# Batch 0's second half of q and k loaded ahead of w_in, transposed before slot 0, and slots 0 to 2 activated on VectorE alone

## The chip, the core and the metric

The kernel runs on one core of one Trainium2 chip. A core has five engines that work side by side and meet at semaphores: TensorE (PE in the profile, with its weight loads as PEld) multiplies matrices into PSUM, VectorE (DVE) and ScalarE (ACT) do elementwise work, GpSimd (POOL) here issues most loads and makes masks, SyncE (SP) issues stores. Loads run on 16 DMA engines that all queues share. The metric is the time of one execution on the device in microseconds (us); before the change its median is 310.11 us over four runs (309.18 to 310.49).

## What is computed

Attention within a band of 32 positions to each side, for 8 batches of 8 heads, 576 positions and head size 64, then a two-layer network with the SMELU activation on the 4608 tokens:

```python
scores = np.matmul(q, k.transpose(0, 1, 3, 2)) / np.sqrt(D)
mask = np.abs(pos[:, None] - pos[None, :]) <= 32
attn = np.exp(np.where(mask, scores, -1e9) - max)      # rows divided by their sums
x = np.matmul(attn, v).transpose(0, 2, 1, 3).reshape(4608, 512)
h = x @ w_in                                           # 512 x 2048
g = np.where(h >= 1, h, np.where(h <= -1, 0.0, (h + 1) ** 2 / 4))
out = g @ w_out                                        # 2048 x 512
```

Inputs and output are float32; the kernel casts q, k, v and the weights to bfloat16 as they are loaded.

## The kernel before

**Slots.** The program is an order written out by hand. After a warm-up comes a loop of slots `a` (L469). A slot takes one block of 256 tokens (`t = a // 8`) and one eighth of the 2048 hidden columns (`f = a % 8`). It multiplies w_in with xT into a PSUM tile `hp` (L491, eight matmuls, called the slot's product here), applies SMELU to hp and writes `gT` (L494 to L503), then does the attention steps listed for this slot (`run(a)`, from the table `ev` that `at` fills, L394 to L413), then one or two pieces of the second layer: a `pair` (L447) or a `quarter` (L431) of eight or four matmuls with w_out. The list `pairs` (L378) gives the slots of the first ten of them.

**SMELU.** With rr = relu(0.5 h + 0.5), slots outside `two_on_act` run rr on ScalarE (L495) and two operations on VectorE, mx = max(h, rr) (L502) and g = min(rr, 1) * mx (L503). Slots in `two_on_act` square rr on ScalarE (L499) and run one operation on VectorE, g = min(max(h, 1), rr^2) (L500). In the first form hp is last read by L502, in the second by L500.

**PSUM.** hp has two buffers in the pool ps_h; slot 6 takes one of ps_o instead (L485). So a slot's product waits until the hp of two slots earlier has been read. ps_s and ps_n have one two-bank buffer each, for scores, sums and transposes. ps_o has two, for the second layer and the last scores of batch 0.

**Attention of a batch.** q and k are loaded by rows and transposed on TensorE for batches 0 and 1 (`tpose`: L187 or L189, and a copy out of PSUM, L190). `scores` multiplies kT with qT (L227; for the first slots a mask is added by L206), and ScalarE takes the exponential (L235, `pt`). `sums` multiplies pt with v and with ones (L293); its `end` takes 1/sum on ScalarE as exp(-ln) (L299 lr, L300 rc), and VectorE's product with it writes xT (L305, L308). These products are put into the list `muls` and are issued at the next `flush()`.

**Warm-up.** q of the first 288 positions comes through SyncE's and ScalarE's queues as float32; everything else comes through GpSimd's queue in the order in which it is issued (L122 to L157). Eight loads may be under way in that queue: each waits for the one eight places before it. The order before is k's first half, v, then line L149: w_in for slots 0 and 1 (`w[:4]`), the second half of q and k (`load_half(1, ...)`), w_in for slots 2 to 6 (columns 1024 to 1536 in two loads of 256 KB, the others in loads of 128 KB); L150: a part of w_out and w_in for slot 7; then three copies on GpSimd that make the masks, used from slot 14 on; more of w_out, and q, k and v of batch 1. The warm-up computes batch 0's scores and sums for the first 256 tokens; `keep_warm` fills in matmuls of zeros. The second half's transposes stand in slot 1 (L394), its scores in slots 2 and 3, its sums in slots 3, 4 and 5.

Of the kernel before, what the change touches and what calls it, by code (L numbers as in the profile page):

```python
# [8 lines left out]
BF = mybir.dt.bfloat16  # L9
AF = mybir.ActivationFunctionType  # L10
ALU = mybir.AluOpType
# [3 lines left out]
def kernel(  # L15
# [20 lines left out]
    B, H, S, D = q.shape  # L36
# [4 lines left out]
    MAIN = 480  # L41
# [13 lines left out]
    ps_h = ctx.enter_context(tc.tile_pool(name="ps_h", bufs=2, space=bass.MemoryType.PSUM))  # L55
    ps_s = ctx.enter_context(tc.tile_pool(name="ps_s", bufs=1, space=bass.MemoryType.PSUM))
    ps_n = ctx.enter_context(tc.tile_pool(name="ps_n", bufs=1, space=bass.MemoryType.PSUM))
# [7 lines left out]
    bias = const.tile([128, 192], BF, name="bias")  # L65
# [8 lines left out]
    V, P, A = nc.vector, nc.gpsimd, nc.scalar  # L74
# [67 lines left out]
    def put(todo):  # L142
        for fn, *x in todo:
            fn(*x)

    w = [(load_w_in, c, c + 256, h) for c in range(0, 1024, 256) for h in range(2)]
    w += [(load_w_in, 1024, 1536, h) for h in range(2)]
    w += [(load_w_in, c, c + 256, h) for c in range(1536, DFF, 256) for h in range(2)]
    put(w[:4] + [(load_half, 1, t, h) for t in range(2) for h in range(2)] + w[4:12])  # L149
    put([(load_w_out, 0, 0, 4)] + w[12:])  # L150
    P.tensor_copy(band[HD[1], 0:128], band[HD[1], 64:192])
    for m, n, x in ((mask4, 8, 128), (mask8, 4, TAIL)):
        P.tensor_copy(m.rearrange("p (n j) -> p n j", n=n),
                      band[:, :x].rearrange("p (n j) -> p n j", n=1).to_broadcast([128, n, x]))
    put([(load_w_out, 0, 4, 8), (load_w_out, 0, 8, 16)] + [(load_rows, 1, t) for t in range(2)])
    put([(load_v, 1, n) for n in range(4)] + [(load_w_out, 1, 8 * n, 8 * n + 8) for n in range(2)])
    put([(load_nat, 2, t) for t in range(2)] + [(load_v, 2, n) for n in range(4)])  # L157

# [3 lines left out]
    def qkT(b, t):  # L162
        if t == 0:
            return qTs[b % 3][:, PAD:]
        if b not in kT:
            kT[b] = ktp.tile([128, NY * S], BF, name="kT")
        return kT[b]

    def tpose(b, n, t, copy, ps):


        half, part = divmod(n, 2)
        j0, j1 = ((0, 5), (5, 9))[part]
        if b:
            src = qn[b] if t == 0 else kn[b]
            src = [src[:, half + 2 * h] for h in range(2)]
            dst = qkT(b, t).rearrange("d (y e p j) -> d y e p j", y=2, e=2, j=9)[:, half, :, :, j0:j1]
            like = "d j (e p) -> d e p j"
        else:
            src = (qn, kn)[t][b, half]  # L180
            src = src if src.shape[1] == 9 else [src[:, h] for h in range(2)]
            dst = qkT(b, t).rearrange("d (y l p j) -> d l y p j", l=2, p=32, j=9)[:, half, :, :, j0:j1]
            like = "d j (p y) -> d y p j"
        for j in range(j0, j1):
            if isinstance(src, list):
                for h in range(2):
                    nc.tensor.transpose(ps[HD[h], j - j0], src[h][:, D * j:D * j + D], ident)  # L187
            else:
                nc.tensor.transpose(ps[:, j - j0], src[:, j], ident)  # L189
        return lambda: copy(dst, ps[:, :j1 - j0].rearrange(like, p=64 if b else 32))  # L190

    def xpose(b, t):

        nc.sync.dma_start_transpose(out=qkT(b, t).rearrange("d (u p) -> d u p", p=128),
                                    in_=(qn, kn)[t][b].rearrange("p u h d -> p (u h d)"))
# [115 lines left out]
    def flush():  # L311
        while muls:
            muls.pop(0)()


    TB = 256

    def tp1(pool):
        if pool is ps_h:
            return pool.tile([128, 8, 128], BF, name="tp", tag="hp")  # L320
        return pool.tile([128, 2, 8, 128], BF, name="tp", tag="bb")[:, 0]
# [10 lines left out]
    def keep_warm(n, pool, tag):  # L332

        z = pool.tile([128, 512], FP, name="z", tag=tag)
        for _ in range(n):
            nc.tensor.matmul(z, warm[:, :128], warm, start=True, stop=True)

    def cast(x, nm, cut):

        y = early.tile([128, 9, 2, D], BF, name=nm)  # L340
        o, i = y.rearrange("p j h d -> p h j d"), x.rearrange("p h (j d) -> p h j d", d=D)
        V.tensor_copy(o[:, :, :cut], i[:, :, :cut])
        A.copy(o[:, :, cut:], i[:, :, cut:])
        return y.rearrange("p j h d -> p j (h d)")

    with tc.tile_pool(name="ps_p", bufs=1, space=bass.MemoryType.PSUM) as ps_p:
        keep_warm(11, ps_h, "hp")

        V.memset(qkT(0, 0).rearrange("d (y s) -> d y s", y=NY)[:, :, S // 2:352], 0.0)
        for b in range(LONG):  # L350
            V.memset(qkT(b, 0).rearrange("d (y s) -> d y s", y=NY)[:, :, S - PAD:], 0.0)
        V.memset(qkT(0, 1).rearrange("d (y s) -> d y s", y=NY)[:, :, S // 2:320], 0.0)
        qn[0, 0] = cast(q32, "qb", 5)
        qq = [tpose(0, n, 0, (A.copy, V.tensor_copy)[n], tp1(ps_h)) for n in range(2)]
        for x in qq:
            x()
        kk = [tpose(0, n, 1, (A.copy, V.tensor_copy)[n], tp1((ps_n, ps_p)[n])) for n in range(2)]
        keep_warm(3, ps_h, "hp")
        for x in kk:
            x()  # L360
        scores(0, (0, 1), (0, 2), (0, 2), None)
        scores(0, (0, 2), (0, 1), (2, 3), None, ps_n, 32)
        scores(0, (1, 2), (0, 2), (0, 2), None, ps_p)
        keep_warm(4, ps_h, "hp")
        e0 = sums(0, 0, 0, TB)
        keep_warm(2, ps_h, "hp")
        e1 = sums(0, 1, 0, TB, ps_p)
        keep_warm(7, ps_h, "hp")
        e0()
        e1()  # L370
    ps_o = ctx.enter_context(tc.tile_pool(name="ps_o", bufs=2, space=bass.MemoryType.PSUM))


# [1 line left out]

    NB = NT // TB
    NF = DFF // 256
    pairs = [(6, 0), (8, 1), (9, 2), (10, 3), (11, 4), (12, 5), (15, 6), (15, 8), (16, 7), (17, 9)]  # L378
    two_on_act = (1, 7, 8, 9, 10, 11, 12)
    ev = {}  # L380

    def at(a, *todo):


        ev.setdefault(a, []).extend(x for x in todo if x)
# [5 lines left out]
                yield (sums, b, y1, lo, hi), (scores, b, (y1, y1 + 1), (0, 2), (2 * k, 2 * k + 2))  # L391
        yield (sums, b, 0, MAIN, S), (scores8, b)

    at(1, (tposes, 0, (0, 1), (1, 1)))  # L394
    at(2, (scores, 0, (0, 1), (0, 2), (2, 4)), (scores8, 0, ps_o))
    at(3, (scores, 0, (1, 2), (0, 2), (2, 4), ps_n), (sums, 0, 0, TB, MAIN, ps_s))
    at(4, (sums, 0, 1, TB, MAIN))
    at(5, (sums, 0, 0, MAIN, S, ps_s))
    seq = [x for b in range(1, B) for x in steps(b, 224)]
    at(13, seq[0][1])  # L400
    at(13.5, (*seq[1][1], ps_n))
    at(14, (*seq[0][0], ps_s), seq[1][0])
    at(16, seq[2][1])
    for n, a in enumerate((18, 20, 22, 28)):
# [10 lines left out]
    for b in range(LONG + 1, B):  # L415
        a = sl[5 * (b - 1) - 7] - 17
# [52 lines left out]
    for a in range(NF * NB + NF):  # L469
        t, f = divmod(a, NF)  # L470
        eng = None if a < 14 else V
        post = [x for n, x in pairs if n == a] + [a - NF] * (a >= 2 * NF + 2)
        for b, x in loads.get(a, []):
            if x < 2:
                load_nat(b, x)
            else:
                for n in range(4):
                    load_v(b, n)
        if a == 0 or a > 3:
            flush()  # L480
        if t < NB:
            if t not in gT:
                gT[t] = gtp.tile([128, 2 * NF, TB], BF, name="gT", tag="gT")
            r0 = TB * t % RING
            if a == 6:  # L485
                hp = ps_o.tile([128, 2, TB], FP, name="hp", tag="op")
            else:
                hp = ps_h.tile([128, 2, TB], FP, name="hp", tag="hp")
            for j in range(2):
                for n, kk in enumerate((0, 2, 1, 3)):  # L490
                    nc.tensor.matmul(hp[:, j], w_in[:, kk, 256 * f + 128 * j:256 * f + 128 * j + 128],  # L491
                                     xT[:, kk, r0:r0 + TB], start=n == 0, stop=n == 3)

            rr = ewp.tile([128, 2, TB], FP, name="rr")  # L494
            A.activation(rr, hp, AF.Relu, scale=0.5, bias=0.5)  # L495
            g = gT[t][:, 2 * f:2 * f + 2]
            mx = ewp.tile([128, 2, TB], FP, name="mx")
            if a in two_on_act:
                A.activation(mx, rr, AF.Square)  # L499
                V.scalar_tensor_tensor(g, hp, 1.0, mx, op0=ALU.max, op1=ALU.min)  # L500
            else:
                V.tensor_max(mx, hp, rr)  # L502
                V.scalar_tensor_tensor(g, rr, 1.0, mx, op0=ALU.min, op1=ALU.mult)  # L503
        flush()
        run(a)
        for x in post:
            (pair if x < 4 * 4 else quarter)(x)
        run(a + 0.5)
        for x in xps.get(a, []):
            xpose(*x)  # L510
# [30 lines left out]
```

The softmax here doesn't subtract the row's maximum and nothing guards it: scores larger than these inputs give would overflow.

## Time and profile before

| What | Value |
|---|---|
| Median of four runs | 310.11 us (309.18 to 310.49) |
| The profiled execution | 310.04 us, of which the span is 308.2 us |
| TensorE busy | 300.3 us (97% of the span) |
| VectorE, ScalarE, GpSimd busy | 242.2, 192.7, 76.8 us |
| Slot 0's product starts | 13.77 us |
| Slot 4's product starts | 23.18 us |
| Granted TensorE clock, mean | 0.997 |

The span runs from the first to the last instruction; the execution has 1.84 us around it. Times below are us from the span's start. In the views a line such as `L491` is a line of the kernel before, `out<-in` are tiles, and a number in brackets is idle time of the engine before the instruction, with what ended it. The rows of digits cut the span into 40 slices of 7.7 us; a digit is the busy share in tenths.

### The profile page before, as it was taken

The numbers are of one execution on the slowest core, as the hardware profiler recorded it, in microseconds if no ns is written. First come the engines' busy times: TensorE is split into PE (matmuls) and PEld (weight loads), VectorE is DVE, ScalarE is ACT, GpSimd is POOL, SyncE is SP. The second block draws the span as 40 slices with busy tenths as digits, with TensorE's granted clock in tenths as the row PEclk, the third lists the DMA queues.
The fourth block names the chain that finished last, engine by engine and source line by source line (L and its number), as shares of the span: only waits on it lengthen the run. The fifth ranks groups of instructions, "written<-read, shape, count | busy, mean of one in ns | idle before, by whom it ended". The sixth has DMA issues, their size and how long they took to land.

```text
span 308.2 us, 8460 instructions
## 1 busy us (share of the span) xinstructions
PE 300.3 (97%) x3634; PEld 205.0 (67%) x3634; DVE 242.2 (79%) x376; ACT 192.7 (63%) x319; POOL 76.8 (25%) x91
## 2 busy tenths in 40 slices
PE   8979999999999999999999999999999999999994
PEld 3558878876666666666666666666666666666651
DVE  4278568978888888889888888889888888887860
ACT  3688786757856667566656666566666666554331
POOL 8798461037009005400460002700000000000000
PEclk9999999999999999999999999999999999999998
DMA  9999999999999989996799055990810001011101
GB/s 153 185 189 193 183 202 154 168 160 158 142 184 111 190 135 98 170 89 145 103 169 142 31 108 89 164 156 17 177 48 36 34 36 36 35 36 40 64 34 68
DMA packets 137013, 35.70 MB, mean 116 GB/s; under 512 B 122128, under 2 KB 132624, under 8 KB 136976
## 3 DMA queue, kind: packets, MB, share of 16 engines
q0 software_dynamic: 102960, 18.06, 82.0%
q1 hardware_dynamic: 33872, 16.81, 24.5%
q8 instruction: 28, 0.46, 0.6%
q10 hardware_dynamic: 144, 0.29, 0.4%
q14 instruction: 9, 0.07, 0.1%
HBM read 36.70 MB, written 9.44 MB: 150 GB/s over the span
## 4 chain that ended last, share of the span: by engine, by line
PE 90%; DMA 4%; POOL 3%; ACT 1%; issue 1%; DVE 0%; POOLq 0%
PE hp L491 39%; PE op L431 37%; PE bb L293 6%; PE op L447 4%; DMA w_in<-in_moe_w_in_dram 4%; PE bb L227 2%; POOL vn L106 1%; POOL w_in L110 1%; PE tp L187 1%; ACT pt L235 1%; POOL kh L85 0%; DVE gT L500 0%; ACT mx L499 0%; PE bb L252 0%; ACT rr L495 0%
## 5 line engine op out<-in xcount | busy, mean ns | idle before, releaser
L491 PE MATMUL hp<-xT,w_in 128*128 128x256 bf16 x1152 | 149.4, 273 | 2.5 <-DVE gT L500 1.1
L495 ACT ACTIVATE rr<-hp 128x512 f32<-128x512 f32 x144 | 85.7, 595 | 88.6 <-PE hp L491 88.6
L491 PEld LDWEIGHTS <-w_in 128*128 128x128 bf16 x1152 | 112.0, 98 | 42.0 <-issue 2.4
L431 PE MATMUL op<-w_out,gT 128*128 128x512 bf16 x512 | 130.4, 380 | 0.0
L502 DVE TENSOR_TENSOR mx<-hp,rr 128x512 f32<-128x512 f32 x137 | 94.5, 690 | 31.6 <-ACT rr L495 29.4
L503 DVE SCALAR_TENSOR_TENSOR gT<-rr,mx 128x512 bf16<-128x512 f32 x137 | 95.2, 695 | 4.7
L431 PEld LDWEIGHTS <-gT 128*128 128x128 bf16 x512 | 47.6, 98 | 36.7
L98 POOL DMA_DIRECT2D qn<-in_q_dram x12 | 14.6, 1224 | 113.1 <-DMA kT<-kn 109.4
L235 ACT ACTIVATE pt<-bb 128x1024 bf16<-128x1024 f32 (+1 forms) x33 | 32.7, 1002 | 4.4 <-PE bb L227 3.0
L305 DVE TENSOR_TENSOR xT<-bb,rc 128x512 bf16<-128x512 f32 (+1 forms) x32 | 21.1, 658 | 10.3 <-ACT rc L300 9.6
L106 POOL DMA_DIRECT2D vn<-in_v_dram x32 | 27.5, 896 | 3.6 <-DMA w_out<-in_moe_w_out_dram 3.3
L436 ACT COPY osb<-op 128x512 f32<-128x512 f32 x32 | 18.7, 583 | 11.8 <-PE op L431 11.3
L300 ACT ACTIVATE rc<-lr 128x512 f32<-128x512 f32 (+2 forms) x40 | 23.5, 587 | 1.3
L299 ACT ACTIVATE lr<-bb 128x512 f32<-128x512 f32 (+2 forms) x40 | 22.1, 551 | 0.4 <-PE bb L293 0.4
L201 DVE TENSOR_TENSOR pt<-pt,mask 128x1024 bf16<-128x1024 bf16 (+1 forms) x33 | 20.3, 614 | 0.2 <-ACT pt L235 0.2
L293 PE MATMUL bb<-pt,ones 64*64 64x256 bf16 (+3 forms) x352 | 19.6, 256 | 0.1
L293 PE MATMUL bb<-pt,vn 64*64 64x128 bf16 (+3 forms) x712 | 18.4, 204 | 0.2 <-DMA vn<-in_v_dram 0.2
L293 PEld LDWEIGHTS <-vn 64*64 64x64 bf16 x712 | 16.7, 107 | 0.4 <-DMA vn<-in_v_dram 0.4
L447 PE MATMUL op<-w_out,gT 128*128 128x256 bf16 x128 | 16.5, 273 | 0.0
L293 PEld LDWEIGHTS <-ones 64*64 64x64 bf16 x352 | 10.2, 105 | 8.6 <-issue 8.6
L98 POOL DMA_DIRECT2D kn<-in_k_dram x12 | 14.6, 1235 | 0.5 <-issue 0.3
L447 PEld LDWEIGHTS <-gT 128*128 128x128 bf16 x128 | 12.0, 98 | 1.9
(56 smaller groups left out, 108.0 us busy)
## 6 DMA issues: line engine op xcount, KB each, us to landing
out_dram<-osb SPq DMA_DIRECT2D x36, 256.0 KB, 2.3
vn<-in_v_dram POOLq DMA_DIRECT2D x32, 144.0 KB, 10.1
qn<-in_q_dram POOLq DMA_DIRECT2D x12, 288.0 KB, 6.7
kn<-in_k_dram POOLq DMA_DIRECT2D x12, 288.0 KB, 9.3
w_in<-in_moe_w_in_dram POOLq DMA_DIRECT2D x12, 128.0 KB, 6.1
w_out<-in_moe_w_out_dram POOLq DMA_DIRECT2D x3, 512.0 KB, 15.3
kh<-in_k_dram POOLq DMA_DIRECT2D x4, 144.0 KB, 5.2
qn<-in_q_dram POOLq DMA_DIRECT2D x1, 576.0 KB, 10.2
```

What stands on the lines that cost most here:

```text
L98: nc.gpsimd.dma_start(out=x[:, :, h], in_=src[b, NY * h:NY * h + NY].rearrange("y s d -> (y s) d") .rearrange("(u p) d -> p u d", p=128))
L106: nc.gpsimd.dma_start(out=vn[b][64 * a:64 * a + 64, :, h], in_=v[b, y:y + 2].rearrange("y s d -> (y s) d") .rearrange("(c r) d -> r c d", ...
L235: A.activation(p, ps[:, :, :w * n].rearrange(like, y=m), AF.Exp, scale=D ** -0.5)
L293: nc.tensor.matmul(bb[HD[h], a, o + c0:o + c1], ones[HD[a]] if c is None else vn[b][HD[a], c, h], p(a, h), start=n == 0, stop=True, skip_g ...
L299: A.activation(lr[:, :, :D0], bb[:, :, D0:2 * D0], AF.Ln)
L300: A.activation(rc[:, :, :D0], lr[:, :, :D0], AF.Exp, scale=-1.0)
L431: nc.tensor.matmul(o, gT[tt // 2][:, j, 128 * (tt % 2):128 * (tt % 2) + 128], w_out[:, j], start=not done, stop=len(done) == 2 * NF - 1, s ...
L447: nc.tensor.matmul(o[:, tt], gT[p][:, j, 128 * tt:128 * tt + 128], w_out[:, j, 256 * half:256 * half + 256], start=not done, stop=len(done ...
L491: nc.tensor.matmul(hp[:, j], w_in[:, kk, 256 * f + 128 * j:256 * f + 128 * j + 128], xT[:, kk, r0:r0 + TB], start=n == 0, stop=n == 3)
L495: A.activation(rr, hp, AF.Relu, scale=0.5, bias=0.5)
L502: V.tensor_max(mx, hp, rr)
L503: V.scalar_tensor_tensor(g, rr, 1.0, mx, op0=ALU.min, op1=ALU.mult)
```

## The change

Four things are done together.

1. GpSimd's queue: the four loads of the second half of q and k go ahead of all of w_in; all of w_in is issued before w_out; the first half of w_out and the row loads of batch 1 are issued ahead of the mask copies.
2. The 36 transposes of the second half and their four copies go into the warm-up, between the sums' ends and slot 0: q's two copies on VectorE, k's two on ScalarE. `keep_warm(7)` becomes `keep_warm(2)`. Batch 0's later steps stand one slot earlier (scores in slots 0 and 1, sums in 2, 3 and 4); the first scores of batch 1 stand in slot 13 behind the pair.
3. Slots 0 to 2 compute SMELU on VectorE alone: rr = max(h, -1) + 1, mx = 0.25 rr^2, g = min(max(h, 1), mx). `two_on_act` becomes 4, 6, 8 to 12.
4. hp of slots 3 and 4 lies in ps_o, that of slot 6 in ps_h. The first six pairs move by about a slot: to slots 7, 8, 10, 11, 12, 13. `flush()` stands ahead of the product in every slot.

```diff
-    put(w[:4] + [(load_half, 1, t, h) for t in range(2) for h in range(2)] + w[4:12])
-    put([(load_w_out, 0, 0, 4)] + w[12:])
+    put([(load_half, 1, t, h) for t in range(2) for h in range(2)] + w)
+    put([(load_w_out, 0, 0, 4), (load_w_out, 0, 4, 8), (load_w_out, 0, 8, 16)] + [(load_rows, 1, t) for t in range(2)])
     P.tensor_copy(band[HD[1], 0:128], band[HD[1], 64:192])
...
-    put([(load_w_out, 0, 4, 8), (load_w_out, 0, 8, 16)] + [(load_rows, 1, t) for t in range(2)])
...
-        keep_warm(7, ps_h, "hp")
+        tp = [pool.tile([128, 2, 8, 128], BF, name="tp", tag="bb") for pool in (ps_s, ps_n)]
         e0()
+        flush()
+        c = [tpose(0, 2 + n, 0, V.tensor_copy, tp[0][:, n]) for n in range(2)]
+        c[0]()
         e1()
+        flush()
+        c[1]()
+        for x in [tpose(0, 2 + n, 1, A.copy, tp[1][:, n]) for n in range(2)]:
+            x()
+        keep_warm(2, ps_h, "hp")
...
-    pairs = [(6, 0), (8, 1), (9, 2), (10, 3), (11, 4), (12, 5), (15, 6), (15, 8), (16, 7), (17, 9)]
-    two_on_act = (1, 7, 8, 9, 10, 11, 12)
+    pairs = [(7, 0), (8, 1), (10, 2), (11, 3), (12, 4), (13, 5), (15, 6), (15, 8), (16, 7), (17, 9)]
+    on_dve = (0, 1, 2)
+    two_on_act = (4, 6, 8, 9, 10, 11, 12)
...
-    at(1, (tposes, 0, (0, 1), (1, 1)))
-    at(2, (scores, 0, (0, 1), (0, 2), (2, 4)), (scores8, 0, ps_o))
-    at(3, (scores, 0, (1, 2), (0, 2), (2, 4), ps_n), (sums, 0, 0, TB, MAIN, ps_s))
-    at(4, (sums, 0, 1, TB, MAIN))
-    at(5, (sums, 0, 0, MAIN, S, ps_s))
+    at(0, (scores, 0, (0, 1), (0, 2), (2, 4)))
+    at(1, (scores8, 0, ps_o), (scores, 0, (1, 2), (0, 2), (2, 4), ps_n))
+    at(2, (sums, 0, 0, TB, MAIN, ps_s))
+    at(3, (sums, 0, 1, TB, MAIN))
+    at(4, (sums, 0, 0, MAIN, S, ps_s))
...
-    at(13, seq[0][1])
-    at(13.5, (*seq[1][1], ps_n))
+    at(13.5, seq[0][1], (*seq[1][1], ps_n))
...
-        if a == 0 or a > 3:
-            flush()
+        flush()
...
-            if a == 6:
+            if a in (3, 4):
...
-            A.activation(rr, hp, AF.Relu, scale=0.5, bias=0.5)
+            if a not in on_dve:
+                A.activation(rr, hp, AF.Relu, scale=0.5, bias=0.5)
...
-            if a in two_on_act:
+            if a in on_dve:
+                V.tensor_scalar(rr, hp, -1.0, 1.0, op0=ALU.max, op1=ALU.add)
+                V.scalar_tensor_tensor(mx, rr, 0.25, rr, op0=ALU.mult, op1=ALU.mult)
+                V.scalar_tensor_tensor(g, hp, 1.0, mx, op0=ALU.max, op1=ALU.min)
+            elif a in two_on_act:
```

## The prediction

> **What bounds the kernel now.** I read the page first, then the chain of waits in order of time, then the timeline and the stretches of the first 50 us. In the page, the row of TensorE (PE) in 40 slices is full from the second slice on, and the row of its granted clock says that nothing is lost to the clock:
>
> ```profile
> PE 300.3 (97%) x3634; PEld 205.0 (67%) x3634; DVE 242.2 (79%) x376; ACT 192.7 (63%) x319; POOL 76.8 (25%) x91
> PE   8979999999999999999999999999999999999994
> PEclk9999999999999999999999999999999999999998
> ```
>
> The stretch from 60 to 297 us has TensorE busy for 237.00 of 237.00 us. So after some 45 us the end is set by TensorE's own work, which the change leaves alone, and only the time at which TensorE reaches a given product can move. The chain of waits shows where it is held up before that:
>
> ```profile
> 8.13 6.42 DMA w_in<-in_moe_w_in_dram
> 16.04 7.00 DMA w_in<-in_moe_w_in_dram
> 23.18 1.03 PE hp L491 x8
> ...
> 30.36 0.70 DVE gT L500
> 31.06 0.04 issue
> 31.10 1.03 PE hp L491 x8
> ...
> 41.59 0.34 PE bb L206 x4
> 41.93 0.05 PE bb L227 x2
> 41.98 0.03 issue
> 42.00 0.43 PE bb L227 x14
> 42.43 0.02 issue
> 42.45 1.95 ACT pt L235 x2
> ```
>
> Columns are start, length, what. Up to 23.05 us the chain is made of w_in landing: slot 4's product (the first that reads the wide columns 1024 to 1536) starts at 23.18. After that there are three short stops, at 31.06 (a PSUM buffer of hp that VectorE frees), 41.98 (a kT copy) and 44.40 (the second exponential of batch 1).
>
> **What the change takes out of the slots.** It moves 36 transposes (1.13 us in the chain at 35.63) and their four copies from slot 1 into the warm-up, and every step of batch 0's attention one slot ahead. At slot 4's product TensorE has one set of sums less to do (24.21 to 24.74: 0.53 us). The transposes lay before 23.18, in time that TensorE spent waiting for w_in, and are worth nothing by themselves. Five fewer keep_warm products (0.24 each by 12.24 to 13.93 for seven) go from a stretch in which TensorE only waits: nothing.
>
> **The loads.** All go through GpSimd's queue in order. The timeline's starts and the times to landing of single issues give: v's last of batch 0 at 5.49+5.2=10.67; the eight that follow (four of w_in, four of q and k, 1088 KB) all by 10.95+5.9=16.89. The change turns the two fours round. By bytes, q and k (576 KB) are then in at 10.67+6.22*576/1088=13.96, slot 0's w_in (832 KB) at 15.4, slot 1's at 16.89 as before. Bounds: the fourth w_in load landed 1.3 us later after its neighbour than the others do, before or after the place in question, so 13.3 to 14.6 and 14.7 to 15.6. Slot 0's product therefore starts at about 15.45 (before: 13.77, held to 14.58 by xT). Behind 16.89 the same bytes stand ahead of the wide w_in. But one thing beside it moves: GpSimd's three copies of the masks.
>
> ```profile
> 19.92 0.29 POOL L151 COPY band<-band 64x128 bf16<-64x128 bf16 x1
> 20.27 1.95 POOL L153 COPY mask<-band 128x1024 bf16<-128x1024 bf16 x2
> 20.79 1.06 DVE L503 SCALAR_TENSOR_TENSOR gT<-rr,mx 128x512 bf16<-128x512 f32 x1
> 22.83 0.69 DVE L503 SCALAR_TENSOR_TENSOR gT<-rr,mx 128x512 bf16<-128x512 f32 x1
> ```
>
> Columns are start, length, engine, line, what. While they run, the queue moves 167 GB/s (stretch 20 to 22) against 199 and 194 in the stretches beside it, and a VectorE operation with both inputs in SBUF takes 1.06 instead of 0.69. After the change they stand behind the two row loads, which wait for the loads eight places earlier (the wide one, and one landed at 16.64+7.2=23.8): about 24.6 to 26.9. So the 30 GB/s lost over 2 us (60 KB, 0.34 us) come back, and I put the wide w_in at 22.7, between 23.05 (nothing comes back) and 21.65, where TensorE would be ready for it (15.45, then four products of 0.87 to 1.03, three steps of scores of 0.52, 0.32 and 0.52, two sums of 0.53, and the wait for slot 1's w_in). The row loads land where they did (23.78+10.2=34.0 and 24.53+12.4=36.9), since the same bytes are ahead and the queue never runs dry; the v of batch 1 is issued some 1.6 us later and lands behind them all the same.
>
> **VectorE in slots 0 to 2.** Each slot has three operations there for two: relu of hp is replaced by a maximum read from PSUM, and hp is read again by the last. ScalarE loses three rr (0.60 each), one square (0.63). The trace has no such tensor_scalar; the nearest rows are the PSUM reads of L502 (0.69) below it and the strided copy L190 (0.73) above it, and 0.55 for the 384 wide L308 as the low end; I take 0.69. A dependent operation starts 0.72 after the one before (22.11 to 22.83), an independent one 0.60 (25.61 to 26.21). Three slots: 3*(0.72+0.72+0.60)=6.12. Then stand in order xT, mx, g of slot 3, xT, g of slot 4, xT, mx of slot 5, with the same steps: 0.54+0.72+0.60+0.54+0.60+0.47+0.69=4.16. Slot 0's result is there 1.07 after its start (23.18 to 24.25), at 16.52: VectorE is busy without a pause until 16.52+10.28=26.80, and 27.17 with 0.37 for one operation under the mask copies. The end of that mx frees the hp buffer that slot 7's product needs, because slots 3 and 4 now sit in ps_o and slot 6 has no filling pair any more. ScalarE reaches the same mx by another way: slot 4 at 22.7, rr at 23.77, square +0.62, lr +0.55, rc +0.52, rr of slot 5 +0.43, 0.60 long, 0.03, mx 0.69: 27.21+0.14 of starting delay (23.05 to 23.18)=27.35. So slot 7 starts at 27.39; TensorE had been ready since 22.84+1.03+0.42+0.87+0.98=26.1.
>
> [...]
>
> **The sum.** From slot 7's start, in steps from the chain: slot 7 1.03, pair 0.87, slot 8 0.87, pair 0.87, slot 9 0.87, wait 0.33 for slot 8's buffer (hp8 at +1.90, rr +0.91, square +0.62, g +0.67, 0.74), slot 10 1.03, pair 0.87, slot 11 0.87, transposes 1.13, pair 0.98, slot 12 0.87, transposes 1.13, pair 0.98, slot 13 0.87, pair 0.87: 14.4. Scores of batch 1 start at 27.39+14.4=41.8, before at 41.59: 0.2 later. The kT wait (0.05) is gone because a pair now lies ahead of the scores; the two exponentials (1.95) still end last. Net +0.15 us on the profiled execution of 310.04 (span 308.2 and 1.84 around it; 0.07 under the median of 310.11): 310.2. In short, the stage gives TensorE 0.5 us of work less after w_in's arrival and a stop at slot 7 in its place, 1.3 us against the stops of 0.3 and 0.4 before.
>
> **Rivals.** *Faster*: slot 7 is held less than worked out. For it: the wide w_in may land by 21.65, the new operation may cost 0.55, slot 0's w_in may be in at 14.7; against it: one of these alone is caught by the other way to slot 7. All together: VectorE 16.52-0.7-0.4+10.28=25.7, ScalarE 27.35-1.05=26.3, slot 7 at 26.35, a gain of 1.0 over the forecast. It then meets a floor: slot 11's transposes (7.6 after slot 7) can't start before the q rows land, 34.0, the k rows at 36.9. That is 309.2, or 308.9 if the rows gain the 0.34 too.
> *Slower*: VectorE's unbroken run from slot 0 to slot 5 is the bound. For it: 10.28 us without a pause, and the mask copies now fall into its last third; against it: only one operation in the trace was stretched by them. If the copies stretch three operations (1.1) and slot 0 starts at 15.65, slot 7 starts at 26.80+1.1+0.2=28.1; with 0.73 for the new operation and a w_in load as late as the 1.3 us straggler, 28.8. Each is later one for one: 310.9 to 311.6. It decides from slot 7 at 28.15 on (+0.93).
> *The clock*: between the q transposes (12.3 to 12.9) and k's arrival TensorE has nothing to do, for 1.1 to 1.7 us, and little until slot 0. If the clock were halved, slots 0 to 3 (some 5 us of work) would take 10 and slot 7 would come 4 us later: 314. The stretch 22 to 24 has TensorE busy for half its time at clock 1.00, which speaks against it. [...]
>
> **How the numbers follow.** The forecast (no change beyond 0.3%, 0.93 us, about what a measurement tells) has 0.46, faster 0.19, VectorE as the bound 0.31, the clock 0.04. The likeliest case's own range is 309.6 to 310.9; to 8 in 10 it reaches into both others: 309.0 to 311.7.
>
> **What would show it.** In the profile after: slot 0's product at 15.4 and slot 4's at 22.7; VectorE without idle time from 16.5 to 27; slot 7's product waiting for VectorE's mx of slot 5 and starting at 27.4; transposes of batch 1's q at 35.0 and its scores at 41.8. Wrong if slot 7's product starts before 26.5 or after 28.2, if a w_in load holds slot 5, 6 or 7, if batch 1's rows hold slots 11 or 12, or if TensorE has idle time after 50 us that it had not before.

## The result, and the profile after

| | Before | After |
|---|---|---|
| Median | 309.55 us (309.06 to 310.73, 75 runs) | 310.39 us (309.73 to 312.23, 50 runs) |
| Profiled execution (span) | 310.04 us (308.2) | 310.06 us (308.3) |
| Slot 0's product starts | 13.77 us | 15.65 us |
| Wide w_in in, slot 4's product starts | 23.05, 23.18 us | 22.70, 22.84 us |
| Slot 7's product starts | 27.99 us | 27.36 us |
| Scores of batch 1, slot 18's product | 41.59, 51.56 us | 41.88, 51.60 us |
| From slot 4's start to the end | 286.86 us | 287.22 us |

The ratio is 1.0025 with a 95% interval of 1.0019 to 1.003: slower, by 0.6 to 0.9 us, which is within the 0.3% called no change here. (The last row of the table is the profiled execution's time less the start of slot 4.) With more runs the median of before came down from 310.11 to 309.55.

The page of the kernel after, engines and slices, where digits are busy tenths:

```profile
PE 299.0 (97%) x3629; PEld 204.4 (66%) x3629; DVE 243.5 (79%) x379; ACT 191.2 (62%) x316; POOL 76.4 (25%) x91
PE   8788999999999999999999999999999999999994
PEclk9999999999999999999999999999999999999999
```

TensorE's work is 1.3 us less than before, nearly all of it the five keep_warm products that are gone, and the span is the same: in the second to fourth slices it is now busy 7, 8 and 8 tenths, where it was 9, 7 and 9. From 60 to 297 us it is busy for 237.00 of 237.00 us as it was before. So all that differs between these two executions lies in the first 50 us. The chain of waits of the kernel after (start, length, what):

```profile
16.03 6.67 DMA w_in<-in_moe_w_in_dram
22.70 0.14 issue
22.84 1.05 PE hp L497 x8
23.91 0.61 ACT rr L502
24.56 0.51 issue
25.07 0.48 ACT lr L298
25.57 0.53 ACT rc L299
26.13 0.56 DVE xT L307
26.69 0.63 DVE mx L513
27.32 0.04 issue
27.36 1.03 PE hp L497 x8
...
41.88 0.34 PE bb L205 x4
42.22 0.25 PE bb L226 x16
42.50 1.95 ACT pt L234 x2
```

The wide w_in comes 0.35 us earlier and slot 4 with it. Then the chain leaves TensorE: it goes through ScalarE's 1/sum (lr, rc), VectorE's product (xT) and the mx of slot 5, whose end frees the hp buffer for slot 7. The timeline of the kernel after (start, length, engine, line, what; in brackets idle time before it and what ended it) shows what that stop costs, and the new operations:

```profile
16.72 0.69 DVE L506 TENSOR_SCALAR rr<-hp 128x512 f32<-128x512 f32 x1 [1.22 <-PE hp L497]
17.45 0.69 DVE L507 SCALAR_TENSOR_TENSOR mx<-rr 128x512 f32<-128x512 f32 x1
18.18 0.69 DVE L508 SCALAR_TENSOR_TENSOR gT<-hp,mx 128x512 bf16<-128x512 f32 x1
...
26.13 0.56 DVE L307 TENSOR_TENSOR xT<-bb,rc 128x384 bf16<-128x384 f32 x1 [0.18 <-ACT rc L299]
...
27.36 1.03 PE L497 MATMUL hp<-xT,w_in 128*128 128x256 bf16 x8 [1.22 <-DVE mx L513]
```

TensorE stands for 1.22 us ahead of slot 7. VectorE's 0.18 us at 26.13 are its only idle time between slot 0's result and that point, so its own unbroken run is almost as late as the way through ScalarE.

### The profile page after: what moved, and what is told of

It reads as the page before. It is cut to its first block, busy times and chain, and to the rows that moved or that the text cites. A ratio compares the mean times of both kernels' runs of the same rounds, so it can differ in the third digit from the quotient of the medians.

```text
span 308.3 us, 8450 instructions
## 1 busy us (share of the span) xinstructions
PE 299.0 (97%) x3629; PEld 204.4 (66%) x3629; DVE 243.5 (79%) x379; ACT 191.2 (62%) x316; POOL 76.4 (25%) x91
## 4 chain that ended last, share of the span: by engine, by line
PE 89%; DMA 4%; POOL 2%; ACT 2%; issue 1%; DVE 1%; POOLq 0%; ACTq 0%
PE hp L497 39%; PE op L438 37%; PE bb L292 6%; PE op L454 4%; DMA w_in<-in_moe_w_in_dram 2%; DMA kh<-in_k_dram 2%; PE bb L226 2%; POOL vn L106 1%; PE tp L186 1%; ACT pt L234 1%; POOL kh L85 0%; ACT rr L502 0%; POOL w_in L110 0%; POOL qh L85 0%; DVE gT L511 0%
## 5 line engine op out<-in xcount | busy, mean ns | idle before, releaser
L502 ACT ACTIVATE rr<-hp 128x512 f32<-128x512 f32 x141 | 83.8, 595 | 86.9 <-PE hp L497 85.5
L513 DVE TENSOR_TENSOR mx<-hp,rr 128x512 f32<-128x512 f32 x134 | 92.5, 690 | 30.5 <-ACT rr L502 28.3
L514 DVE SCALAR_TENSOR_TENSOR gT<-rr,mx 128x512 bf16<-128x512 f32 x134 | 92.7, 692 | 4.6
L98 POOL DMA_DIRECT2D qn<-in_q_dram x12 | 14.6, 1222 | 113.1 <-DMA kT<-kn 109.4
L98 POOL DMA_DIRECT2D kn<-in_k_dram x12 | 14.6, 1234 | 0.7 <-issue 0.4
```

The costliest lines, as they stand in the source:

```text
L98: nc.gpsimd.dma_start(out=x[:, :, h], in_=src[b, NY * h:NY * h + NY].rearrange("y s d -> (y s) d") .rearrange("(u p) d -> p u d", p=128))
```

## The experiments

Eleven sets of runs were made: both kernels again and nine other kernels, each beside runs of the kernel before on the same chip. "Ratio" is to those, with its 95% interval.

**Both kernels again.** No edit.

> The kernel before, unchanged, for a second profile. Both theories start from the same question: the two profiled executions end within 0.02 us of each other, while the medians over 75 and 50 runs stand 0.84 us apart. Theory A (landing): the profiled execution of before was an unlucky one, in which the wide w_in load for slot 4 landed at 23.05; here it lands earlier, by 22.5, slot 4's product starts by 22.6 and the time is 309.3 to 309.7. Theory B (nothing special): slot 4 again starts at 23.1 to 23.2 and the time is about 310.0.

> The kernel after, unchanged. Both theories: 0.2 to 0.3 per cent above before. Theory A: slot 7's product starts no earlier than 27.2 even if the wide w_in lands early, because VectorE's run from slot 0 to slot 5 ends there. Theory B: slot 7's start follows slot 4's one for one, and the difference of the medians lies behind 45 us.

Before: 309.48 us, ratio 0.9996 [0.9981, 1.0011]. After: 310.29 us, ratio 1.0017 [1.0003, 1.003]. In the profile of the first the wide w_in landed at 23.80 (execution of 310.62); in that of the second at 22.48, slot 7 at 27.19 (309.90). A single profiled execution of the same kernel thus lies up to 1.1 us off the median, and most of that is when w_in lands: from slot 4's start on, before takes 286.69 and 286.86, after 287.22 and 287.28. The early landing that the first theory expected in the profile of before did not show, and neither did the second theory's 23.1. In the second profile of after slot 4 starts 0.22 us earlier than in the first and slot 7 only 0.17 us earlier, and the last operations ahead of slot 7 follow each other on VectorE alone (g of slot 4, xT, mx of slot 5): the two ways to slot 7 lie within 0.2 us of each other.

**The stop at slot 7.** The kernel after, with slot 7's hp in ps_o as well.

```diff
-            if a in (3, 4):
+            if a in (3, 4, 7):
```

> After, with slot 7's hp in the pool ps_o, so that its product needn't wait for VectorE's read of slot 5's hp. Theory (VectorE's run holds slot 7 by its PSUM buffer, 1.2 us in the profile after): slot 7 starts at 26.1 to 26.3, nothing later takes it back before the row loads of batch 1 (33.5 and 36.4 against 35.05 and 38.03), and the time is 0.7 to 1.2 us below after: 309.2 to 309.7, some 0.1 per cent below before. Rival (the same VectorE and ScalarE work only moves the stop to slots 8 to 10): the time is that of after, within 0.3 us.

309.40 us, ratio 0.9985 [0.9972, 0.9997]; 0.89 below the kernel after on the same chip (310.29). The timeline of this kernel has slots 5, 6 and 7 as one piece of 24 matmuls:

```profile
24.46 2.79 PE L497 MATMUL hp<-xT,w_in 128*128 128x256 bf16 x24
```

With the buffer wait gone, slot 7 starts at 26.22, though slot 4 began at 23.08, later than in the profile after. The two intervals stand apart: the stop is worth the change's whole loss, and without it the change is slightly faster than before.

**SMELU on VectorE alone, taken back.** The kernel after, with slots 0 to 2 on ScalarE and VectorE.

```diff
-    on_dve = (0, 1, 2)
+    on_dve = ()
```

> After, with slots 0 to 2 activated as before (rr on ScalarE, two operations on VectorE); nothing else. Theory (VectorE's three operations a slot hold slot 7, and ScalarE's own way to the same operation is only 0.1 to 0.2 us shorter): VectorE's run is 2 us shorter, ScalarE has 1.8 us more, slot 7 starts at 27.0 to 27.4 and the time is within 0.3 us of after. Rival (the three operations alone are the loss): slot 7 starts at about 26.2 and the time falls by 0.8 to 1.2 us.

310.03 us, ratio 1.0013 [1.0, 1.0026]. The chain of waits of this kernel:

```profile
23.22 1.05 PE hp L497 x8
...
25.45 0.48 ACT lr L298
25.95 0.53 ACT rc L299
26.51 0.56 DVE xT L307
27.07 0.63 DVE mx L513
27.70 0.04 issue
27.74 1.03 PE hp L497 x8
```

Slot 7 still comes 4.52 us after slot 4, exactly as in the profile after (27.36 less 22.84). VectorE stands idle in between in this kernel (0.91 us and 0.24 us, the latter ended by rc), so ScalarE's way alone holds slot 7, and the time is within 0.3 us of after: that the three VectorE operations are the whole loss is refuted.

**The mask copies.** Once the kernel after with the copies back ahead of the second w_out load, once the kernel before with them behind the row loads. The first edit (the second moves the last line of this diff the other way, ahead of the copies):

```diff
-    put([(load_w_out, 0, 0, 4), (load_w_out, 0, 4, 8), (load_w_out, 0, 8, 16)] + [(load_rows, 1, t) for t in range(2)])
+    put([(load_w_out, 0, 0, 4)])
     P.tensor_copy(band[HD[1], 0:128], band[HD[1], 64:192])
...
+    put([(load_w_out, 0, 4, 8), (load_w_out, 0, 8, 16)] + [(load_rows, 1, t) for t in range(2)])
```

> After, with GpSimd's three mask copies put back ahead of the second and third part of w_out, as in the kernel before. Theory A, the prediction's step (the copies slow the load queue and so delay the wide w_in load by 0.34 us): the load lands at 23.0 to 23.4 where after has 22.5 to 22.9, slot 4 starts later by 0.3, and the time is 0.2 to 0.4 us above after. Theory B (that load's landing varies by itself, 22.5 to 23.1 in four profiles with late copies, and the copies have no part in it): the time is within 0.2 us of after.

> Before, with the mask copies behind the row loads of batch 1, as after has them; nothing else. Theory A: 0.2 to 0.4 us below before. Theory B: within 0.2 us of before.

Copies early in the kernel after: 310.43 us, ratio 1.0020 [1.0003, 1.0037]. Copies late in the kernel before: 309.88 us, ratio 1.0001 [0.9989, 1.0012]. The stretch from 20 to 22 us of the kernel after with the copies early, so with the copies in it; columns are the busy time of the five engines with counts, TensorE's clock, the load of the DMA engines and, last, their GB/s:

```profile
20.00:22.00 2.00, 2.00 (x52) 1.44 (x53) 1.93 (x4) 1.31 (x3) 1.90 (x4) 1.00 1.21 166
```

The same stretch of the kernel before with the copies late, so without them:

```profile
20.00:22.00 2.00, 2.00 (x72) 1.56 (x65) 1.38 (x2) 1.92 (x5) 1.46 (x3) 1.00 1.32 191
```

These two agree with the prediction's reading, but two other kernels do not. The kernel of the next experiment has the copies in this stretch (19.93 to 21.76 us), and the kernel with SMELU on VectorE taken back has none before 25 us:

```profile
20.00:22.00 2.00, 1.12 (x35) 0.68 (x34) 1.99 (x4) 1.19 (x4) 1.94 (x4) 1.00 1.33 188
20.00:22.00 2.00, 2.00 (x65) 1.61 (x64) 1.53 (x3) 1.97 (x5) 1.60 (x3) 1.00 1.21 168
```

Over the ten profiles with the wide w_in load the stretch moves 139 to 188 GB/s with the copies in it and 168 to 196 without, so the copies alone do not set this rate. The wide w_in lands at 22.96 to 23.80 in the four profiles with early copies and at 22.48 to 23.08 in the six with late ones, which leans the prediction's way and overlaps. The timed runs can't tell: neither edit moves the median by more than its interval, and a term of 0.34 us, 0.11%, is not excluded by them either (for the kernel before it lies at the edge, 0.9989).

**The order of the loads alone.** The kernel before, with only the second half of q and k moved ahead of w_in.

```diff
-    put(w[:4] + [(load_half, 1, t, h) for t in range(2) for h in range(2)] + w[4:12])
+    put([(load_half, 1, t, h) for t in range(2) for h in range(2)] + w[:12])
```

> Before, with the second half of q and k loaded ahead of w_in; its transposes stay in slot 1, and all else stays. Theory (slot 0 can't start before its w_in at 15.5, and everything up to slot 4 stands behind it): slot 0 starts at 15.5 to 15.8, slot 1 at 17.0, its transposes and copies end after 19, slots 2 and 3 follow with their scores, and slot 4 starts at 23.3 to 24.0, after its w_in has landed: 0.3 to 0.9 us above before. Rival (slot 4 is held by its w_in alone, and all before it has room): within 0.2 us of before.

310.93 us, ratio 1.0035 [1.0023, 1.0047]. Slot 0 starts at 15.62 and slot 4 at 23.94, 0.98 after its w_in landed (22.96), because w_in for slots 0 and 1 comes later now, and with it slot 1 and the transposes, copies and scores that TensorE still has to pass ahead of slot 4. In its chain of waits:

```profile
20.10 0.68 DVE qT L190
20.77 0.65 DVE kT L190
21.43 0.04 issue
21.47 0.45 PE bb L227 x16
```

So the new order costs 0.35% by itself. Whether the rest of the change gives a part of that back is not shown: the whole change has 1.0019 to 1.003, which overlaps.

**Two stops removed.** The kernel after with slot 7's hp in ps_o, and batch 1's first scores ahead of slot 13's pair, which then covers the exponentials.

```diff
-    at(13.5, seq[0][1], (*seq[1][1], ps_n))
+    at(13, seq[0][1], (*seq[1][1], ps_n))
...
-            if a in (3, 4):
+            if a in (3, 4, 7):
```

> After, with slot 7's hp in ps_o, and both first scores of batch 1 ahead of slot 13's pair. Theory: slot 7's stop of 1.2 us and the stop of 0.4 us before the sums of slot 14 are gone, 0.3 to 0.4 us below the kernel that has slot 7's hp in ps_o alone: 308.9 to 309.2, 0.2 to 0.3 per cent below before. Rival (the row loads of batch 1, 34.06 and 37.01 against transposes at 34.18 and 37.16 in that kernel, or v of batch 1 and w_out take the place of the stop): no gain over it.

308.99 us, ratio 0.9970 [0.9958, 0.9983]. The exponentials (1.95 us in the chain after) no longer hold TensorE. The interval overlaps that of slot 7's hp alone in ps_o (0.9972 to 0.9997), so the gain of this second step is not clear of noise. What comes next is in its chain:

```profile
23.67 13.11 DMA kn<-in_k_dram
36.78 0.04 issue
36.82 1.20 PE tp L186 x36
```

The k rows of batch 1, landed at 36.78, now hold the transposes (TensorE stands 0.19 us): the floor that the prediction's faster case named.

**The wide w_in cut in four.** The two loads of 256 KB for slots 4 and 5 become four of 128 KB, so that slot 4 waits for half the bytes; in the kernel before, in the kernel after, and in the kernel with both stops removed.

```diff
-    w += [(load_w_in, 1024, 1536, h) for h in range(2)]
+    w += [(load_w_in, c, c + 256, h) for c in (1024, 1280) for h in range(2)]
```

In the kernel before the slices `w[4:12]` and `w[12:]` become `w[4:14]` and `w[14:]`, so that the order stays.

> Before, with the wide w_in load for slots 4 and 5 (two of 256 KB) cut into four of 128 KB, those of slot 4 first. Theory (slot 4 waits for this landing, and from slot 4's start to the end of the execution it is 286.7 to 286.9 us in every profile of this slot order): slot 4's w_in lands 1.2 us earlier, slot 4 starts when TensorE is ready, at 22.1 to 22.4, and the time is 309.0 to 309.3, 0.3 to 0.5 us below before. Rival (something else holds slot 4 or the slots behind it in the timed runs): within 0.2 us of before.

> After, with the same cut. Theory: slot 4 starts at 22.1 to 22.4 and the rest takes 287.25 us, so 309.4 to 309.7, 0.3 to 0.5 us above the cut kernel before: with the landing out of the way the difference is that of the stretch from slot 4 on. Rival A (VectorE's run holds slot 7 at 27.2 whatever slot 4 does): 309.9 to 310.2, 0.8 us above the cut kernel before. Rival B (the two are level): 309.0 to 309.3.

> The fastest kernel so far (slot 7's hp in ps_o, batch 1's first scores ahead of slot 13's pair), with the same cut. Theory (the k rows of batch 1 hold slot 12's transposes by now: landed at 36.78, transposes at 36.82 in that kernel's profile): within 0.2 us of that kernel, 308.8 to 309.1. Rival (slot 4 still decides): 308.3 to 308.6.

In the kernel before: 310.64 us, ratio 1.0026 [1.0012, 1.0041], which neither theory had. Slot 4 does start at 22.30. But its chain of waits then goes through GpSimd's queue:

```profile
23.18 0.69 POOL w_out L115
23.87 8.61 DMA w_out<-in_moe_w_out_dram
32.47 0.04 issue
32.52 1.03 PE op L447 x8
```

The third part of w_out lands at 32.47 (31.13 in the profile before), the pair of slot 9 that reads it waits, and slot 10 starts at 33.38 (32.84 before). Why it lands late is open. The bytes ahead of it are the same, and the load ahead of it landed at 28.06, earlier than in the profile before (28.52); but the stretches 26 to 28 and 28 to 30 move 147 and 164 GB/s where the profile before has 193 and 208, and the kernel with the same cut below has it at 31.09.

In the kernel after: 309.87 us, ratio 1.0006 [0.9997, 1.0015]. That is just under the range of rival A (309.9 to 310.2), whose mechanism the chain shows: slot 4 starts at 22.32, and slot 7 nevertheless at 27.36.

```profile
17.02 0.70 DVE rr L506
...
26.25 0.47 DVE xT L307
26.71 0.61 DVE mx L513
27.32 0.04 issue
27.36 1.03 PE hp L497 x8
```

Nothing of ScalarE decides here: VectorE's own run from slot 0's result to the mx of slot 5 does. Both ways to slot 7 are real, and either alone is enough to hold it.

In the kernel with both stops removed: 308.37 us, ratio 0.9963 [0.9950, 0.9976], the lowest of all, though the interval overlaps that of the uncut kernel (0.9958 to 0.9983). Slot 4 starts at 22.01 and slot 7 at 25.71. In its chain:

```profile
22.87 0.62 DVE xT L304
23.50 0.04 issue
23.54 0.49 PE bb L292 x19
```

So the rival's number came (308.3 to 308.6) but not its reason: slot 4 no longer waits for w_in, and it is VectorE's run from slot 0 on, up to this xT, for which TensorE stands 0.48 us behind slot 4's product.

## Why the prediction was right, step by step

The forecast was 310.2 us and no change beyond 0.3%; measured are 310.39 us and +0.25%. The path was right: slot 0 later, slot 4 earlier, a new stop at slot 7. That the totals agree so well is in part luck. The forecast started from an execution of 310.04 us, 0.49 above the median that more runs gave, and its own difference of +0.15 us stands against 0.84 between the medians; the 0.3% (0.93 us) was nearly used up.

- *Loads ahead of slot 0.* Put at 15.45, measured at 15.65. Two things hold it alike. k landed at 14.54 against the 13.96 worked out by bytes (and within the 14.6 of the bound) and held the k transposes (0.77 us of idle time), 1.11 us ahead of slot 0. Slot 0's w_in was in at 15.52, and slot 4's product starts 0.14 after its own landing, which gives 15.66 here. In the two profiles where w_in came later against k (the copies early in the kernel after, and the cut load there; 15.82 and 15.81 with k at 14.66 in both) slot 0 starts 0.14 behind w_in.
- *VectorE's three operations.* Priced at 0.69 each from the nearest PSUM read; measured 0.69, 0.69, 0.69. The place of the source made no difference: L506 reads PSUM, L507 only SBUF, and both took 0.69.
- *The stop at slot 7.* Put at 27.39, with TensorE ready at 26.1; measured 27.36 and an idle time of 1.22, so ready at 26.14. The two ways, 26.80 to 27.17 by VectorE and 27.35 by ScalarE, both exist: the cut kernel after shows the one, the kernel without VectorE's SMELU the other.
- *From slot 7 to the scores.* 14.4 worked out, 14.52 measured (41.88 less 27.36). The q transposes came at 35.05 (35.0). The kT stop, put at 0.05, was worth more: from the scores' start to the first exponential before took 42.45 less 41.59, 0.86, after 42.50 less 41.88, 0.62. So 0.24 came back there, and the exponentials end only 0.05 later than before.
- *From slot 4 to the end.* The forecast had +0.49 (0.15 net and 0.34 of earlier landing taken off). Measured: 287.22 and 287.28 after against 286.86 and 286.69 before, that is +0.36 to +0.59.
- *The mis-sized term: the 0.34 us that w_in gains from the moved mask copies.* The profile after has the landing of the forecast (22.70), but that the copies are its cause is not shown: the rate of the queue, from which the 0.34 us were worked out, does not follow the copies in every profile (188 GB/s with them, 168 without). Putting them back cost the kernel after 0.04 us in its median (310.43 against 310.39), and moving them away brought the kernel before nothing (1.0001, with 0.9989 the lower end, which is a gain of 0.34). The profile before was an execution in which w_in landed late. The kernel's median of 309.55 less the 286.86 from slot 4 on puts slot 4 at 22.7 (an estimate, no row shows it), where the forecast has it only with the credit. The credit was taken from one execution's loads and set against the median of others.
- *The 0.37 us for a VectorE operation stretched by the mask copies* did not come. The copies ran from 25.03 on; the one operation of that stage with both inputs in SBUF, L514, ran at 24.13 and took 0.69.

The rivals. *Faster*, 308.9 to 309.2, needed slot 7 at 26.35: that is what putting slot 7's hp in ps_o makes (26.22, 309.18 in its profile, 309.40 in the median), so the price was about right and the condition absent. *VectorE as the bound* needed slot 7 from 28.15 on; VectorE's run was 0.18 short of deciding even at 27.36. *The clock*: TensorE stood for 0.77 us at most between the q transposes and slot 0, and the clock's row stayed at 9 in every slice. A halved clock stands at the end of the profile before, 0.50 from 307.0 us on, behind the last product (ended at 304.30); in the profile after, with the last product ended at 304.34, it is 1.00 to the end.

What stays open is the last part of the median's +0.84. Of it some 0.4 to 0.6 are the stretch from slot 4 on. For the rest there are two readings, and no run decides between them. One: two ways to slot 7 that are equal in one execution and scatter from run to run give the later of the two in every run, and the prediction took them as one time, 27.39. Take ScalarE's way out of the kernel after (the cut load) and it has 309.87; take VectorE's way out and it has 310.03; take both out and it has 309.40; with both it has 310.39. But the interval without VectorE's way (1.0 to 1.0026) overlaps that with both. The other: w_in for slot 4 lands later in the timed runs of the kernel after than in its two profiles; 310.39 less 287.22 puts slot 4 at 23.2 (an estimate), against 22.7 in the kernel before. The cut load takes out that landing too, so it fits either reading. The timed runs leave no trace in which this could be read.

## What to carry to other kernels

A buffer that is handed round (here two for hp) moves with every slot whose buffer or filling is changed: after such an edit, look for the product whose buffer is freed last, since one entry in a list of slots (7) was worth 0.9 us here and decided the sign. When two ways end at the same wait within a few tenths, taking one of them out gains little there: slot 7 came 4.52 us after slot 4 with VectorE's three operations and without them. And a term of a few tenths that rests on when a load landed in one profiled execution is to be tested against the timed runs before it goes into a sum: here the same load landed between 22.5 and 23.8 us in profiles of kernels that differ little.

## What the runs showed of the hardware

**Loads landed over 1 us late beside a packet of another queue.** In the profile before a w_in load lands at 14.55, 1.97 us after its neighbour; in the profile after a k load lands at 14.54, 1.74 after; the other neighbours come 0.25 to 0.8 apart. In both profiles one thing from outside falls into that time. The DMA queues from 12.4 to 13.6 us in the kernel after (packets, MB, share of 16 engines):

```profile
q0 software_dynamic: 372, 0.22, 129.1%
q8 instruction: 1, 0.02, 4.7%
```

The same stretch of the profile before has one such packet too, with 5.1%. One packet of instructions, 4.7% of 16 engines for 1.2 us, would be 0.9 us if it lay on one engine, against some 0.07 for a packet of the loads (129.1% of 19.2 us over 372); both are estimates from these rows. Both late loads were the fourth of their group; in the second profile of the kernel before it is the third (14.19, 2.16 after its neighbour), so the place in the group does not decide. That the packet is the cause is only read from its place in time, and it is no rule: in the profile before another such packet (4.6% of 16 engines from 22.7 to 24 us) has loads landing at 23.82 and 24.47 beside it, 0.77 and 0.65 after their neighbours, as usual. No run moved the first packet.

**GpSimd's copies and VectorE slowed each other only for some operations.** In the timeline of the kernel after with the copies early:

```profile
20.71 1.48 POOL L153 COPY mask<-band 128x1024 bf16<-128x1024 bf16 x2
21.85 0.88 DVE L508 SCALAR_TENSOR_TENSOR mx<-rr 128x512 f32<-128x512 f32 x1
```

VectorE's other operations under that copy read PSUM and took their usual 0.68 and 0.69; this one, whose inputs are both in SBUF, overlapped the copy's last 0.34 us and took 0.88. In the kernel before g (L503, both inputs in SBUF) lay wholly under the copies: 1.06, and the copies took 1.95 for 1.48. In the kernel before with the copies late, it is a later g that lies under them: 0.94 and 1.95. In the kernel with the order alone changed, g fell behind the copies: 0.69 and 1.48. In these rows the stretched operations are those with both inputs in SBUF; what stretches them is not shown.
